# A spectral filter and two mixtures on one core: the first mixture's product with w_k in seven block products over pairs of chunks

## The chip, the cores and the metric

One core of a Trainium2 chip runs the whole kernel as one launch. The metric is the time of the device in microseconds (us). Lower is better.

## What is computed

The reference has three parts, one after the other, all in float32, for x of 8 batches, 3072 positions and 256 channels:

```python
y = irfft(rfft(x, axis=1) * (filt_r + 1j * filt_i), n=3072, axis=1)

prev = y moved by one position, 0 in front
xk = mu_k * y + (1 - mu_k) * prev
xr = mu_r * y + (1 - mu_r) * prev
k = relu(xk @ w_k)                      # 256 x 1024
x2 = sigmoid(xr @ w_r) * ((k * k) @ w_v)    # 256 x 256, 1024 x 256

h = max(x2 @ w1, x2 @ w2, x2 @ w3)      # 256 x 768 each
out = h @ w_out                         # 768 x 256
```

## The kernel before

**Products.** An fp32 product is made of three matmuls of a rounded type (fp32r): each operand is split into a hi and a lo part, and hi x hi, hi x lo and lo x hi are added up in a bank of PSUM (`mm3`, lines 155 to 163). `split` (line 177) makes the parts: ScalarE casts the hi part, and GpSimd (or VectorE, where it is named) subtracts it from the source for the lo part. Line 153 is the one line that issues every matmul, so the profile's groups are told apart by tile names.

**The transform** of a batch (`fft`, from line 328) runs in steps of small products through two buffers in DRAM, s1 and s2: 17 pieces that read x and write s1 (tiles xa, pa, ao), then 28 that read s1 (xb, pb), multiply with the filter, and write s2 (pc, co). Batch 0 has a version of its own (`fft_first`, line 420), in which the orders of TensorE, ScalarE and the DMA queue of SyncE are written by hand. Between its steps it also starts the conversion of the weights, which come as 64-bit numbers: a job is a triple of load, narrow (ScalarE, five VectorE operations, GpSimd) and parts. `CONV` and `LOAD` say at which step which job runs.

**The first mixture** works on chunks of 4 x 96 = 384 positions, 64 chunks in all. `y_load` and `y_mm` (lines 572, 583) bring a chunk's last transform step (py, yt) and make xk and xr (xm, then parts xh and xl). `r_mm` (line 613) makes the gate. `k_mm` (line 623) makes one of eight blocks of 128 columns of k: six matmuls, relu on ScalarE, the square on VectorE, the split. `v_mm` (line 636) follows three blocks behind: six matmuls into the two banks pv, with w_v's parts from DRAM. The parts of w_k stay on the chip. `x2` multiplies v by the gate.

**The second mixture** (`second`) takes two chunks at a time. `combos` (line 655) makes the sums of x2 that a product of 2 x 2 blocks by seven block products needs (Winograd's form), `block` (line 683) does the seven products of one of nine blocks (three fq, three of w1, w2 and w3), with the sums of the weights read from DRAM (wud). In it bank b collects products 1, 2, 4 and 6, and ScalarE copies it between them (pa, u, v); bank a takes product 3, bank e products 5 and 7. `out` takes the maximum (m), and `o_mm` (line 754) does the product with w_out in three banks po that stay open through the stage.

**The order.** The stages are lists of units with weights. In the steady part a pair of chunks is: first mixture of an even chunk, second mixture, first mixture of an odd chunk, sums. `drive` (line 108) lays the pieces of the next batch's transform between the units in proportion to their weights. Outside the hand-written parts the framework's planner then orders each engine's instructions by a simulated timeline. All tiles of PSUM come from one pool of eight banks (tag pm). Weights from DRAM go through one ring of buffers (`ws`), asked for eight loads ahead in the order of `later` and `piece_of` (lines 256 to 267), on SyncE's queue.

## Time and profile before

| | us |
|---|---|
| median of 3 runs | 3241.59 (3240.01 to 3244.37) |
| the profiled execution | 3234.65 |
| its span, first to last instruction | 3232.9 |
| TensorE busy in the span | 3117.1 (96%) |
| ScalarE / GpSimd / VectorE busy | 1918.4 / 1870.1 / 1839.3 |
| data moved by DMA | 676.38 MB |

The profile is one execution. PE is TensorE's matmuls, PEld its weight loads, DVE VectorE, ACT ScalarE, POOL GpSimd, SP SyncE. Times in a group are the sum of its busy time, the mean of one instruction in ns, and the idle time of the engine just before them with what ended it. Matmuls are pipelined, so the recorded length of one is longer than the distance to the next.

### The profile page before, as it was taken

How to read it: one execution, taken by the hardware profiler on the slowest of the kernel's cores; microseconds unless marked ns; L12 is line 12 of the kernel's file. 1: busy time of each engine (PE TensorE's matmuls, PEld its weight loads, DVE VectorE, ACT ScalarE, POOL GpSimd, SP SyncE). 2: the span in 40 equal slices, each digit the busy share in tenths (PEclk: the TensorE clock that was granted, in tenths of full speed). 3: DMA queues.
4: the chain of work that ended last, by engine and by line, in shares of the span. 5: the costliest groups of instructions: out<-in, count | busy, mean ns of one | idle time of the engine just before them, and what ended most of it. 6: DMA issues, size and time to landing. Idle time of an engine off the chain costs nothing.

```text
span 3232.9 us, 55814 instructions
## 1 busy us (share of the span) xinstructions
PE 3117.1 (96%) x19256; PEld 3040.1 (94%) x19256; DVE 1839.3 (57%) x2882; ACT 1918.4 (59%) x4024; POOL 1870.1 (58%) x1619
## 2 busy tenths in 40 slices
PE   7799899999999999999999999999999999999998
PEld 4799899999999999999999999999999999999998
DVE  4865565566555665566545565556654566555554
ACT  5556556666656666656666556565656566555554
POOL 3545665666555775556656566566665566544443
PEclk8899999999999999999999999999999999999999
DMA  8767786667765776657766677666776667655553
GB/s 283 234 227 218 246 298 186 193 200 245 225 195 183 230 225 204 208 185 243 233 191 189 206 241 233 192 185 203 254 226 192 190 211 226 190 171 159 163 167 119
DMA packets 397783, 676.38 MB, mean 209 GB/s; under 512 B 41920, under 2 KB 153664, under 8 KB 396864
## 3 DMA queue, kind: packets, MB, share of 16 engines
q1 hardware_dynamic: 328336, 585.61, 58.4%
q10 hardware_dynamic: 66752, 78.75, 7.1%
q0 software_dynamic: 2416, 8.46, 0.9%
q8 instruction: 156, 2.56, 0.3%
q14 instruction: 123, 1.01, 0.1%
HBM read 580.51 MB, written 92.14 MB: 208 GB/s over the span
## 4 chain that ended last, share of the span: by engine, by line
PE 82%; DMA 7%; DVE 6%; issue 2%; POOL 2%; ACT 1%; SPq 0%; ACTq 0%; POOLq 0%; DVEq 0%
PE pb L153 17%; PE pk L153 15%; PE pv L153 14%; PE po L153 12%; PE pe L153 8%; PE pa L153 7%; PE pr L153 4%; DMA ws<-wud 3%; PE py L153 3%; PE pc L153 2%; DVE xm L604 1%; POOL klo L179 1%; DMA xb<-s 1%; DVE sc L662 1%; DMA s<-ao 1%
## 5 line engine op out<-in xcount | busy, mean ns | idle before, releaser
L153 PE MATMUL pb<-x,ws 128*128 128x384 f32 x3456 | 749.1, 338 | 23.4 <-ACT v L698 8.4
L179 POOL TENSOR_TENSOR hh<-m,hh 128x384 fp32r<-128x384 f32 x384 | 400.5, 1048 | 610.6 <-ACT hh L178 497.4
L179 POOL TENSOR_TENSOR klo<-kr,khi 128x384 fp32r<-128x384 f32 x492 | 515.6, 1056 | 208.7 <-ACT khi L178 192.0
L153 PEld LDWEIGHTS pb<-x,ws 128*128 128x128 f32 x3456 | 595.9, 188 | 38.4 <-ACT v L698 10.5
L630 DVE SCALAR_TENSOR_TENSOR kr<-pk,kr 128x384 f32<-128x384 f32 x512 | 281.1, 552 | 489.5 <-ACT kr L629 489.4
L153 PE MATMUL pv<-khi,ws 128*128 128x384 f32 x2048 | 480.7, 337 | 6.7 <-ACT khi L178 6.7
L153 PE MATMUL po<-wo_hi,hh 128*128 128x256 f32 x2304 | 480.9, 283 | 3.8 <-ACT hh L178 2.8
L153 PE MATMUL pe<-x,ws 128*128 128x384 f32 x1728 | 389.8, 338 | 14.2 <-DVE m L737 10.7
L153 PEld LDWEIGHTS po<-wo_hi,hh 128*128 128x128 f32 x2304 | 391.1, 190 | 7.0 <-ACT hh L178 5.1
L153 PEld LDWEIGHTS pv<-khi,ws 128*128 128x128 f32 x2048 | 360.0, 188 | 11.6 <-ACT khi L178 10.1
L178 ACT CAST khi<-kr 128x384 fp32r<-128x384 f32 x512 | 261.0, 512 | 164.9 <-DVE kr L630 148.3
L153 PE MATMUL pk<-xh,wk_hi 128*128 128x384 f32 x1024 | 342.0, 337 | 3.9 <-ACT xh L178 3.9
L153 PE MATMUL pk<-xl,wk_hi 128*128 128x384 f32 x1024 | 344.3, 336 | 0.2 <-DVE xl L179 0.2
L153 PE MATMUL pk<-xh,wk_lo 128*128 128x384 f32 x1024 | 344.0, 336 | 0.0
L745 DVE TENSOR_TENSOR m<-sc,m 128x384 f32<-128x384 f32 x384 | 315.6, 828 | 7.3
L153 PEld LDWEIGHTS pe<-x,ws 128*128 128x128 f32 x1728 | 300.4, 189 | 20.1 <-DVE m L737 12.1
L153 PE MATMUL po<-wo_lo,hh 128*128 128x256 f32 x1152 | 317.0, 282 | 0.0
L629 ACT ACTIVATE kr<-pk 128x384 f32<-128x384 f32 x512 | 250.0, 489 | 109.9 <-PE pk L153 49.0
L178 ACT CAST hh<-m 128x384 fp32r<-128x384 f32 x384 | 194.7, 514 | 200.2 <-DVE m L745 142.2
L153 PE MATMUL pv<-klo,ws 128*128 128x384 f32 x1024 | 300.3, 339 | 10.0 <-POOL klo L179 8.9
L179 POOL TENSOR_TENSOR xl<-xm,xh 128x768 fp32r<-128x768 f32 x126 | 235.6, 1883 | 67.4 <-ACT xh L178 64.7
L604 DVE SCALAR_TENSOR_TENSOR xm<-yt,nmu_s,xm 128x384 f32<-128x384 f32 x256 | 210.7, 857 | 97.1 <-ACT xm L603 96.9
(129 smaller groups left out, 6065.9 us busy)
## 6 DMA issues: line engine op xcount, KB each, us to landing
ws<-wud SPq DMA_DIRECT2D x864, 256.0 KB, 3.4
ws<-wvd SPq DMA_DIRECT2D x512, 256.0 KB, 3.5
filt<-in_filt SPq DMA_DIRECT2D x84, 512.0 KB, 5.4
ws<-wud SPq DMA_DIRECT2D x288, 128.0 KB, 3.4
wbc<-wbcd SPq DMA_DIRECT2D x72, 512.0 KB, 4.7
cin<-s SPq DMA_DIRECT2D x64, 384.0 KB, 4.2
out_dram<-osb ACTq DMA_DIRECT2D x192, 128.0 KB, 3.1
xb<-s SPq DMA_DIRECT2D x85, 256.0 KB, 3.5
```

Source lines behind the costliest of these rows:

```text
L153: nc.tensor.matmul(o, lhsT=wgt, rhs=rhs, start=start, stop=stop, skip_group_check=more)
L178: nc.scalar.copy(hi, src)
L179: (lo_eng or nc.gpsimd).tensor_tensor(lo, src, hi.bitcast(F32), ALU.subtract)
L604: nc.vector.scalar_tensor_tensor(v[:, h], yt[:, h, :, :MC], nmu_s[:, w, h : h + 1], v[:, h], ALU.mult, ALU.add)
L629: nc.scalar.activation(r, p, AF.Relu)
L630: nc.vector.scalar_tensor_tensor(r, p, 0.0, r, ALU.max, ALU.mult)
L662: eng.tensor_tensor(t, a, b, ALU.subtract)
L745: nc.vector.tensor_tensor(m, c, m, ALU.max)
```

## The change

The first mixture takes pairs of chunks too. `combos` is made general (for `xk` and `x2`), and so is the code of the seven products (`seven`): `k_block` does one of four blocks of 256 columns of w_k for two chunks. Two of its four outputs are relu and square as before, the other two are first a sum of a bank and a copy, then relu and square on ScalarE. The sums of w_k are made during the transform of batch 0 (`block_job`, which had served w1 to w3) and are read from DRAM for each pair. `v_half` does half of a v product; w_v is loaded once for both chunks, and v has four banks. The units of a block of k are laid between the v halves of the block before; the last block's v halves go into the first block of the second mixture, and the y and r units of the pair after next into its blocks 0, 2, 3, 5, 6 and 7. The order is now: first mixture of pair p+1, second mixture of pair p, with the sums of x2 for p+1 after the first block of pair p+2. The transform's side list has a pause of weight 6 after the first load of its second step. Some buffers change in number (ws, xh, xl, yt, khi, klo, gate).

```diff
...
-    ws = ctx.enter_context(tc.tile_pool(name="ws", bufs=10))
+    ws = ctx.enter_context(tc.tile_pool(name="ws", bufs=9))
...
+    eye = cpool.tile([P, 2, P], F32, name="eye")
+    nc.scalar.dma_start(eye, ones)
...
+    wk_d = [dp.tile([P, 7, 2, P], F32, tag=f"wkd{k}", name=f"wkd{k}", bufs=1) for k in range(NF // 2)]
...
-        fq, j = divmod(k, 3)
+    def block_job(src, kt, q, to, queue):
...
+                queue.dma_start(to[:, a:e], t.bitcast(F32))
+        return piece(src, kt, 0, 2, 2 * P * q, 2 * P * (q + 1), parts)
...
-    wk = weight("wk", w_k, 2, DF)
...
-    wjobs1 = wk[2] + [wv_job(q) for q in range(NF // 2)] + wr[2]
+    wjobs1 = [block_job(w_k, 2, q, wk_d[q], nc.gpsimd) for q in range(NF // 2)] + wr[2]
+    wjobs1 += [wv_job(q) for q in range(NF // 2)]
...
+            if s == 0:
+                pieces.append((6.0, lambda: None))
             pieces.append((0.65, pc))
...
                 jobs[k][1](False)
-                jobs[k][2](False)
...
+            if s in CONV or s == 11:
+                jobs[CONV.get(s, 5) - 1][2](False)
...
-            e = mp.tile([NQ, C], F32, tag="cprev", name="cprev", bufs=1)
+            e = mp.tile([NQ, C], F32, tag="kr", name="cprev")
...
-        yt = mp.tile([P, 2, NP, MC + 1], F32, tag="yt", name="yt")
+        yt = mp.tile([P, 2, NP, MC + 1], F32, tag="yt", name="yt", bufs=1)
...
+            nc.gpsimd.tensor_copy(yt[:, :, :, 0], cs["y"])
+        if (i + 1) % NCH:
+            cs["y"] = mp.tile([P, 2, NP], F32, tag="yl", name="ylast", bufs=1)
+            nc.gpsimd.tensor_copy(cs["y"], yt[:, :, :, MC])
...
+            v = mp.tile([P, 2, NP, MC], F32, tag="xm", name="xm", bufs=3)
...
+            v = v.rearrange("p h t m -> p h (t m)")
+            if name == "k":
+                cs["k", i] = v
+            else:
+                hi = mp.tile([P, 2, NT], F32R, tag="xh", name="xh", bufs=1)
+                lo = mp.tile([P, 2, NT], F32R, tag="xl", name="xl", bufs=1)
+                split(hi, lo, v)
+                cs["r", i] = hi, lo
...
-        g = mp.tile([P, 2, NT], F32, tag="gate", name="gate", bufs=3)
...
-    def k_mm(i, f):
-        xh, xl = cs["k", i]
...
-        mm3(p, [(wk[0][:, k, s], wk[1][:, k, s]) for k in range(2)], [(xh[:, k], xl[:, k]) for k in range(2)])
-        r = mp.tile([P, NT], F32, tag="kr", name="kr")
-        nc.scalar.activation(r, p, AF.Relu)
-        nc.vector.scalar_tensor_tensor(r, p, 0.0, r, ALU.max, ALU.mult)
-        hi = mp.tile([P, NT], F32R, tag="khi", name="khi", bufs=LAG + 1)
-        lo = mp.tile([P, NT], F32R, tag="klo", name="klo", bufs=LAG + 1)
-        split(hi, lo, r, nc.vector if i == 0 or i < 4 and f % 2 else None)
...
+    def v_half(c, f, h, first, last, at):
+        kh, kl = cs["s", c, f]
+        if first:
+            cs["pv", c, h] = ps.tile([P, NT], F32, tag="pm", name="pv")
+        p = cs["pv", c, h]
         w = piece_of(at)
-        for h in range(2):
-            p = cs["pv"][h]
-            s = slice(h * P, (h + 1) * P)
-            mm(p, w[:, 0, s], kh, f == 0, False)
-            mm(p, w[:, 1, s], kh, False, False)
-            mm(p, w[:, 0, s], kl, False, f == NF - 1)
+        s = slice(h * P, (h + 1) * P)
+        mm(p, w[:, 0, s], kh, first, False)
+        mm(p, w[:, 1, s], kh, False, False)
+        mm(p, w[:, 0, s], kl, False, last)
...
-            nc.vector.tensor_tensor(g[:, h], cs["pv"][h], g[:, h], ALU.mult)
...
+            nc.vector.tensor_tensor(g[:, h], cs["pv", i % 2, h], g[:, h], ALU.mult)
+    def combos(name, ga, gb):
...
-            t = mp.tile([P, 2, NT], F32R, tag=f"x2_{k}", name="x2", bufs=1)
+            t = mp.tile([P, 2, NT], F32R, tag=f"{name}_{k}", name=name, bufs=1)
             split(t[:, 0], t[:, 1], v, eng)
-            cs["x2", k] = t[:, 0], t[:, 1]
+            cs[name, k] = t[:, 0], t[:, 1]
...
-    def block(p, k, at):
...
+    def comb_k(p):
+        combos("xk", cs.pop(("k", 2 * p)), cs.pop(("k", 2 * p + 1)))
+    def comb_x2(p):
+        combos("x2", cs.pop(("g", 2 * p)), cs.pop(("g", 2 * p + 1)))
+    def seven(name, at, out):
         st = {}
         def prod(o, n, onto):
             t = piece_of(at[n][0])[:, at[n][1]]
-            mm3(o, [(t[:, 0], t[:, 1])], [cs["x2", n]], onto, True)
+            mm3(o, [(t[:, 0], t[:, 1])], [cs[name, n]], onto, True)
...
-        def seven():
...
+        return [one, two, three, four, five, six, last]
+    def k_block(k, at):
+        def out(n, q, add=None):
+            r = mp.tile([P, NT], F32, tag="kr", name="kr")
+            if add is None:
+                nc.scalar.activation(r, q, AF.Relu)
+                nc.vector.scalar_tensor_tensor(r, q, 0.0, r, ALU.max, ALU.mult)
+            else:
+                c = mp.tile([P, NT], F32, tag="sc", name="sc", bufs=4)
+                nc.vector.tensor_tensor(c, q, add, ALU.add)
+                nc.scalar.activation(r, c, AF.Relu)
+                nc.scalar.activation(r, r, AF.Square)
+            hi = mp.tile([P, NT], F32R, tag="khi", name="khi", bufs=6)
+            lo = mp.tile([P, NT], F32R, tag="klo", name="klo", bufs=6)
+            split(hi, lo, r)
+            cs["s", n // 2, 2 * k + n % 2] = hi, lo
+        return seven("xk", at, out)
...
+    def u_block(k, at):
+        fq, j = divmod(k, 3)
...
+    def y_units(p):
+        i = 2 * p
+        return [
+            (0.0, lambda: y_load(i)),
+            (1.3, lambda: (y_mm(i), y_load(i + 1))),
+            (1.95, lambda: r_mm(i)),
+            (1.3, lambda: y_mm(i + 1)),
+            (1.95, lambda: r_mm(i + 1)),
+            (0.0, lambda: comb_k(p)),
+        ]
...
+    def kv(p, before=(), y=(), after=()):
...
+        for k in range(NKB + 1):
+            if k < NKB:
+                ask(wk_d[k], at[k], 0, 2)
+            if k:
+                av[2 * k - 2] = later(wv_d[k - 1][:, 0], 2, C)
+            if k < NKB:
+                ask(wk_d[k], at[k], 2, 4)
+            if k:
+                av[2 * k - 1] = later(wv_d[k - 1][:, 1], 2, C)
+            if k < NKB:
+                ask(wk_d[k], at[k], 4, 5)
+                ask(wk_d[k], at[k], 5, 7)
+        order = [(0, 0), (1, 1), (0, 1), (1, 0)]
+        for k in range(NKB + 1):
+            fill = []
+            if k:
+                for c, f in order:
+                    first = k == 1 and (c, f) in order[:2]
+                    end = k == NKB and (c, f) in order[2:]
+                    f += 2 * k - 2
+                    for h in range(2):
+                        fill.append((0.52, lambda c=c, f=f, h=h, first=first, end=end: v_half(c, f, h, first, end, av[f])))
+                    if end:
+                        fill.append((0.0, lambda c=c: x2(2 * p + c)))
+            else:
+                fill = before
+            if k == NKB:
+                return u, fill
+            for fn in k_block(k, at[k]):
+                u.append((0.52, fn))
+                if fill:
+                    u.append(fill.pop(0))
+            u += fill
+            u += y[2 * k - 2 : 2 * k] if k else list(after)
+    def second(p, before=()):
...
+        todo = list(before)
+        y = dict(zip((0, 2, 3, 5, 6, 7), y_units(p + 2))) if 2 * p + 4 < NTOT else {}
...
+            if k in y:
+                u.append(y[k])
...
+            now = u_block(k, at[k])
...
+                for _ in range(3 if k == 0 else n in ((3,), (0, 2, 3), (0, 1))[k % 3]):
+                    if todo:
+                        u.append(todo.pop(0))
...
+            if k == 0:
+                u += todo
+                todo = []
...
+        late = [(0.52, fn) for fn in late]
+        return u, late, [(0.71, lambda q=q: o_mm(p, NU // 2 - 1, q)) for q in range(2 * NTB)]
...
-        mm(p, wk[0][:, 0, :P], wk[0][:, 0, :NT], True, True)
-    wjobs1[8][0]()
+        mm(p, wr[0][:, 0, :P], wr[0].rearrange("p k n -> p (k n)")[:, :NT], True, True)
     y_mm(0)
-    eye = mp.tile([P, 2, P], F32, tag="osb", name="eye")
-    nc.sync.dma_start(eye, ones)
-    for k in (5, 6, 7, 8):
+    y_load(1)
+    r_mm(0)
+    y_mm(1)
+    comb_k(0)
+    r_mm(1)
+    for k in range(5, 9):
+        if k > 6:
+            wjobs1[k][0]()
         wjobs1[k][1]()
         wjobs1[k][2]()
...
-    units = kv(0) + kv(1) + kv(2) + [(0.0, lambda: combos(0))] + kv(3)
...
+    sums = lambda p: [(0.0, lambda: comb_x2(p))]
+    units, tail = kv(0, y=y_units(1)[:4])
+    first2 = len(units)
+    units += tail + y_units(1)[4:]
+    u, tail = kv(1, after=sums(0))
+    units += u
...
+    starts = [0]
+    for p in range(NPAIR):
+        if (2 * p + 4) % NCH == 0 and 2 * p + 4 < NTOT:
+            starts.append(len(units))
+        u, late, left = second(p, tail)
+        units += u
+        if p + 2 < NPAIR:
+            u, tail = kv(p + 2, late + left, after=sums(p + 1))
+            units += u
+        elif p + 1 < NPAIR:
+            units += late + sums(p + 1)
+            tail = left
+    units += late + left
+    lead2 = (first2 + 2 * before2) // 3
...
+            drive(part, side, sum(w for w, _ in part), sum(w for w, _ in side))
...
```

## Rows read from the trace of the kernel before

**Rows 1.** The page: the span, and busy time, share and instructions of each engine.
```profile
span 3232.9 us, 55814 instructions
...
PE 3117.1 (96%) x19256; PEld 3040.1 (94%) x19256; DVE 1839.3 (57%) x2882; ACT 1918.4 (59%) x4024; POOL 1870.1 (58%) x1619
```

**Rows 2.** Windows: stretch, busy time per engine (instructions), granted clock, DMA share, GB/s.
```profile
0.00:100.00 100.00, 64.82 (x197) 42.46 (x198) 48.90 (x69) 45.98 (x73) 43.63 (x42) 0.83 0.88 282
...
2800.00:2900.00 100.00, 100.00 (x635) 100.00 (x634) 52.09 (x87) 57.57 (x126) 49.44 (x46) 1.00 0.55 165
...
1180.00:1192.00 12.00, 12.00 (x75) 12.00 (x74) 3.58 (x7) 8.08 (x18) 10.08 (x9) 1.00 0.64 209
...
1216.00:1228.00 12.00, 11.02 (x69) 10.70 (x68) 7.91 (x15) 5.62 (x15) 3.60 (x4) 1.00 0.87 307
```

**Rows 3.** The chain that ended last: start, length in us, what.
```profile
140.00 3.12 PE ps L153 x28
...
2891.83 3.12 PE pk L153 x18
...
2978.69 3.12 PE pk L153 x18
```

**Rows 4.** Waits of TensorE, 600 to 3100 us: total us, times, longest.
```profile
PE pe L153 <- DVE m L737: 8.8, 6, 1.5
PE pv L153 <- POOL klo L179: 8.5, 12, 1.1
PE pb L153 <- ACT v L698: 8.4, 6, 1.7
PE pb L153 <- DMA ws<-wud: 5.4, 8, 1.4
PE pa L153 <- DMA ws<-wud: 5.2, 8, 1.0
PE pb L153 <- PE pe L153: 3.8, 6, 0.6
```

**Rows 5.** Groups: one of the three kinds of k matmul.
```profile
L153 PE MATMUL pk<-xh,wk_hi 128*128 128x384 f32 x1024 | 342.0, 337 | 3.9 <-ACT xh L178 3.9
```

**Rows 6.** TensorE's timeline at the start of the first mixture: start, us, what.
```profile
98.14 3.70 PE L153 MATMUL py<-wi_s,cin 96*128 96x96 f32 x16 [12.34 <-DMA cprev<-s]
...
106.57 1.65 PE L153 MATMUL pk<-xh,wk_hi 128*128 128x384 f32 x4 [3.87 <-ACT xh L178]
```

**Rows 7.** DMA: the total, then issues with their count, size and us to landing.
```profile
DMA packets 397783, 676.38 MB, mean 209 GB/s; under 512 B 41920, under 2 KB 153664, under 8 KB 396864
...
ws<-wvd SPq DMA_DIRECT2D x512, 256.0 KB, 3.5
...
cin<-s SPq DMA_DIRECT2D x64, 384.0 KB, 4.2
```

**Rows 8.** Groups of VectorE: a product and a sum out of PSUM, a sum in SBUF.
```profile
L630 DVE SCALAR_TENSOR_TENSOR kr<-pk,kr 128x384 f32<-128x384 f32 x512 | 281.1, 552 | 489.5 <-ACT kr L629 489.4
...
L744 DVE TENSOR_TENSOR sc<-pe,u 128x384 f32<-128x384 f32 x192 | 106.2, 553 | 69.5 <-PE pe L153 68.5
...
L662 DVE TENSOR_TENSOR sc<-gate 128x384 f32<-128x384 f32 x32 | 44.6, 1394 | 0.0
```

**Rows 9.** ScalarE's timeline where the transform of a batch starts its second step.
```profile
1410.85 0.62 ACT L178 CAST xbh<-xb 128x512 fp32r<-128x512 f32 x1 [2.51 <-DMA xb<-s]
1411.38 0.47 ACT L698 COPY v<-pb 128x384 f32<-128x384 f32 x1
1411.74 0.48 ACT L698 COPY u<-pb 128x384 f32<-128x384 f32 x1
```

**Rows 10.** Groups of ScalarE: the relu of k and one of the three copies.
```profile
L629 ACT ACTIVATE kr<-pk 128x384 f32<-128x384 f32 x512 | 250.0, 489 | 109.9 <-PE pk L153 49.0 <-POOL klo L179 41.5 <-POOL xbl L179 7.4
...
L698 ACT COPY u<-pb 128x384 f32<-128x384 f32 x288 | 138.7, 481 | 76.2 <-PE pb L153 75.4
```

**Rows 11.** Groups of GpSimd: the lo parts of k.
```profile
L179 POOL TENSOR_TENSOR klo<-kr,khi 128x384 fp32r<-128x384 f32 x492 | 515.6, 1056 | 208.7 <-ACT khi L178 192.0 <-DMA ws<-wud 6.9 <-PE pv L153 3.3
```

More of the change, by code (lines that the diff above doesn't have):

```diff
@@ L750, in out @@
                 cs["h", fq, n // 2, n % 2] = t
-        return [one, two, three, four, five, six, seven]
+        return seven("x2", at, out)
     def o_mm(p, fq, k):
@@ L812, in second, with ask @@
-    def second(p):
+    def ask(d, at, a, e):
+        i = later(d[:, a:e], e - a, 2, P)
+        at.update({n: (i, n - a) for n in range(a, e)})
+    def y_units(p):
[9 more added lines that the diff above has]
+    def kv(p, before=(), y=(), after=()):
+        u = []
+        before, y = list(before), list(y)
+        NKB = NF // 2
+        at = [{} for _ in range(NKB)]
+        av = {}
+        for k in range(NKB + 1):
[32 more added lines that the diff above has]
+            u += y[2 * k - 2 : 2 * k] if k else list(after)
@@ L902, in tile_spectral_moe @@
         part = units[starts[b] : ends[b]]
+        if b == 0:
+            for _, fn in part[:lead]:
+                fn()
+            part = part[lead:]
         if b + 1 < B:
             side = fft(b + 1)
-            cut = cuts[b] + n2 - starts[b]
-            if b == 0:
-                for _, fn in part[:lead]:
-                    fn()
-                part, cut = part[lead:], cut - lead
-            drive(part[:cut], side, sum(w for w, _ in part[:cut]), sum(w for w, _ in side))
-            for _, fn in part[cut:]:
-                fn()
+            drive(part, side, sum(w for w, _ in part), sum(w for w, _ in side))
         else:
```

111 lines of the change are left out of this document (15 added, 96 removed).

## The prediction

> **What bounds the kernel now.** I read the engine totals first [rows 1]: TensorE is busy for 3117.1 of 3232.9 us, and no other engine is above 59%. Then the windows [rows 2]: the first 100 us hold only 65 us of TensorE work at a granted clock of 0.83, and a window late in the run, where no transform runs beside the mixtures, is full (100.00 of 100) at clock 1.00. So the time is TensorE's stream of matmuls plus a start-up of its own kind. The price of a matmul comes from the chain in order of time [rows 3]: 18 matmuls of 384 columns take 3.12 us, so one takes 0.1733 us, and two pieces of the same place in the loop lie 86.83 us apart (2978.69 less 2891.83): one pair of chunks without a transform. The per-instruction mean of 335 to 338 ns in the groups is the length of a pipelined record, about twice the spacing; it must not be used as the price.
>
> The waits of TensorE between 600 and 3100 us [rows 4] sum to 40.1 us in 2500: the steady part is 98.4% full. About half of it lies, by the timeline, where the first mixture of an odd chunk hands over to the second mixture: late lo parts of k (8.5 us) and late w1/w2/w3 products from DRAM (5.4 + 5.2 us). The rest is one place per batch where ScalarE holds a copy back (8.4 us) and one where VectorE does (8.8 us), with 3.8 us put down to its own earlier products.
>
> **The change, part by part.**
>
> *w_k by seven block products.* A pair of chunks needed 2 x 8 x 6 = 96 matmuls of 384 columns; the groups have 1024 of each of three kinds [rows 5], 3072 in 32 pairs. Now four blocks of 7 x 3 = 21 make 84. Removed: 12 x 32 = 384, times 0.1733 us: **66.6 us** off the full engine. The number of v products stays (48 a chunk); only their order and the banks change.
>
> *Preparing the sums of w_k.* Four jobs are added, each of 28 matmul records like the preparation of w1 in the same chain: 3.12 us each [rows 3], 12.5 us, in the transform of batch 0, where TensorE's order is written by hand and was free of such work. TensorE has holes there, so not all of it is paid. Bounds 0 and 12.5; I take **+8**, nearer the upper end, since the order is fixed and each job's matmuls wait for its own conversion.
>
> *The start of the first mixture.* Before, the first k product starts 8.4 us after the first y product (106.57 less 98.14) [rows 6]. Now the sums xk need both chunks: y of chunk 1 waits for its load into a single buffer (`cin`, 4.2 us to landing [rows 7]) and for the one `yt` to come free, then four sums in a row on VectorE (0.55 to 1.39 us each [rows 8]) come before the second product. The r products of both chunks (24 x 0.1733 = 4.2 us) move there and fill part. The first block has nothing between its products. Lower end: one load, paid back by the r products, 0. Upper end: the load, the 8.4 us from y to the first product once more, and four sums at 1.39 us, 18. The four w_v jobs now all stand behind y, and the first v product waits for them. I take **+8**, near the middle, as the load is certain and the sums may hide behind r.
>
> *Handing over between stages.* The last v products of a pair now run among the first products of the second mixture, and the sums x2 are made a whole stage before they are used, so the two waits that made up 19.1 us (8.5 + 5.4 + 5.2 [rows 4]) lose their place. Late k parts can still occur, since the same four-step chain stands behind each v product; I take **-15**, bounds 0 and -19. The side work gets a pause of weight 6 between its first and second step: there the transform reads back what it has just written, and ScalarE stands 2.51 us at the cast of it before it comes to a copy that TensorE needs [rows 9]; of the 8.4 us of such copies I take **-6**, bounds 0 and -8.4.
>
> *ScalarE in a k block.* An output now costs more there: per block three copies out of PSUM, two relus from PSUM, two relus and two squares out of SBUF, four casts: 13 instructions, where the same 7.8 us of TensorE (21 + 24 matmuls, 45 x 0.1733) held 7.5. In the timeline [rows 9] two copies start 0.36 us apart, though the groups record 0.48 or 0.49 for each [rows 10]; with 0.4, an estimate for the mix with the longer casts, 13 make 5.2 us of 7.8, 67%, with the transform's casts and those of x2 on top. The window of today's first mixture shows 8.08 of 12 us, that of the second 5.62 [rows 2]. ScalarE stays under TensorE, but each product on bank b waits for a copy of it, as in the second mixture today. The waits there that name copies, sums and earlier products (8.8 + 8.4 + 3.8 = 21 us [rows 4]) fell in about 26 stages of 9 blocks (2500 us at some 97 us a pair), 0.09 us a block; for the 128 new blocks **+12**, bounds 0 (v products between them give more cover than today's) and 50 (0.4 us, one ScalarE place, in each).
>
> *VectorE.* Two of the four outputs of a block now take a sum out of PSUM (0.553 us) where they took a product out of PSUM (0.552) [rows 8]: nothing changes. The sums for xk are new: 7 instructions a pair (four sums, three lo parts), between 0.55 us (the PSUM form) and 1.39 us (the same form with both inputs in SBUF), 3.9 to 9.8 us, and they stand in the last three of nine blocks of the second mixture, together with the x stage of a chunk. The 0.55 would be the price without GpSimd beside it. VectorE has the cover on average (57%), but it is there that it holds TensorE back today. I take 0.3 us a pair, **+10**, bounds 0 and 62 (2.0 us a pair; the longest such wait of today is 1.5 [rows 4]).
> The page "SBUF — State Buffer" of the Trainium skill, section "Who interferes with whom", says that a VectorE instruction with two SBUF inputs and a GpSimd instruction that reads SBUF exclude each other for the whole instruction. The trace agrees (1394 ns against 553); by that rule the xk sums cost GpSimd their length too, which is the second rival.
>
> *GpSimd.* The lo parts of k (1056 ns [rows 11]) stay 16 a pair; for the x of k four of that size replace two of twice the elements, beside TensorE: costed at nothing. Where this cover is gone it shows as a wait for klo.
>
> *DMA.* w_v once a pair: 256 of 512 loads of 256 KB go, 67 MB. w_k comes in: 32 x 4 blocks of 7 x 128 KB, 117 MB; with 676 MB before [rows 7], +7%. SP issues 60 weight loads a pair for 52. The first mixture's demand goes from 4.2 MB in the time of 192 matmuls (33.3 us, 126 GB/s) to 5.8 MB in that of 180 (31.2 us, 185 GB/s), still under the 307 GB/s of a window of the second [rows 2]. One `ws` buffer fewer leaves eight loads ahead. Costed at nothing; without that cover a late load is 0.65 us on the mean and 1.4 at most [rows 4].
>
> The sum: -66.6 + 8 + 8 - 15 - 6 + 12 + 10 = -49.6 us. It is made on the profiled execution (3234.65 us, 1.75 us around its span), which is 7 us under the median of the three runs shown; against that median, 3241.59, it gives **3192 us**.
>
> **The rivals.**
>
> *The dovetailing takes all.* The preparation fits the holes and no new wait appears: -66.6 + 4 - 19 - 8.4 = -90, 3152 us. For it: late windows show the engine 100.00% full with the same kind of blocks. Against it: ScalarE and VectorE get some 17% and 12% more work (25 instructions of 0.4 us and 7 of about 1 us a pair).
>
> *VectorE and GpSimd at the end of the second mixture.* If the seven xk sums run at 1.39 us and the outputs of block 6 and 7 queue behind them, banks stay taken and TensorE stops about 2 us a pair: +62 in place of +10, 3244 us, no change. For it: VectorE waits are the largest entry of today's list [rows 4]. Against it: two blocks of the second mixture still lie between these sums and their first use, and each of today's waits is one per batch, not per pair.
>
> *PSUM, on the slow side.* From the second block on, v holds four of the pool's eight banks, and b and e of the last block with b and a of the new one are the other four; the transform needs one as well. Bank b comes free a relu and a product after the sixth product (0.49 [rows 10] + 0.55 us [rows 8], with a place in the queue 1.4), and product seven with two v parts (9 matmuls) cover 1.56. If ScalarE is three instructions behind (1.2 us), TensorE stops for about 1.05 us in 96 blocks: +101 in place of +12, 3281 us, slower. It decides from (49.6 + 12 + 6.5) / 96 = 0.71 us a block. Against it: the second mixture of today holds three banks of `po` besides its blocks and stops little.
>
> That the products don't fall away can't be: the three kinds of `pk` matmul are gone from the code.
>
> **How the numbers follow.** The forecast as summed, 0.49; all taken, 0.27; VectorE, 0.15; PSUM, 0.09. A measurement here tells 0.2%, 6.5 us, from no change. Faster by more: 0.49 + 0.27 and 0.07 of the VectorE case, **0.83**; within: 0.06 of that case; slower: 0.02 of it and PSUM, **0.11**. The range runs from 3150 (the first rival) to 3240 (preparation and start-up at their upper bounds, +14.5, none of the hand-over waits gone, +21, and 0.7 us a pair for the xk sums, +12); outside lie PSUM, half of the VectorE case and a little below, 0.2.
>
> **What would show it.** Right: `pk` records are replaced by 2688 in banks of b, a and e, TensorE's busy time falls by about 54 us, klo and `ws` waits fall under 10 us together, ScalarE rises to about 70% of the span. Wrong: a wait for a copy or a bank that comes back four times a pair (PSUM); waits for `m` in the last blocks of the second mixture (VectorE); the first block of k more than 30 us later than 106 us (start-up). A pair without transform that takes more than 86 us instead of 84.8 (86.83 less 12 x 0.1733) would refute the main term.

## The result and the profile after

The changed kernel takes 3285.97 us (median of four runs, 3283.08 to 3292.98) against 3240.8 us for the kernel before in the same comparison: a ratio of **1.0143 (95% interval 1.0131 to 1.0156)**, so 1.4% slower. 3192 us was forecast. The profiled execution of the changed kernel took 3292.98 us, 7 us over its median, and that of the kernel before 7 us under its own; so the two spans (3291.2 and 3232.9 us) differ by 58.3 us where the medians differ by 45.

The totals of the changed kernel's page, beside [rows 1]:

```profile
span 3291.2 us, 57217 instructions
...
PE 3108.8 (94%) x18984; PEld 2995.3 (91%) x18984; DVE 2063.2 (63%) x3086; ACT 2241.3 (68%) x4830; POOL 1982.0 (60%) x1765
```

272 matmuls fell away (384 less 112 of the w_k preparation), yet TensorE's busy time fell by 8.3 us only. A matmul's record is longer than its spacing (some 337 ns against 174 for 384 columns), and a short stall inside a string of them is counted as busy. So I priced every matmul at the median distance from its start to the next start (384 columns 0.1735 us, 256 columns 0.119, the transform's 512 columns 0.234, y 0.111, preparation 0.112), called the sum *work*, and what is left of the time up to the last matmul *lost*:

| | work | lost | of it up to 500 us | 500 to 2800 | behind |
|---|---|---|---|---|---|
| before | 3033.8 | 193.2 | 115.7 | 66.7 | 10.8 |
| changed | 2979.7 | 305.7 | 156.8 | 126.2 | 22.7 |
| difference | -54.1 | +112.5 | +41.1 | +59.5 | +11.9 |

The work fell by 54 us, which is the removed products and the whole of the preparation (-66.6 + 12.5), and twice as much was lost again: 41 us in the start, 60 us in the steady part. The Trainium skill's page "Perfetto Trace Analysis", section "Identifying the Most-Contended Engine", says that matmul busy time is not a good measure of how close a kernel is to the limit, because matmuls are pipelined, and names the rate of work done (MFU) and the weight loads' busy time in its place. This case agrees for the latter: PEld fell by 44.8 us and came far nearer the 54.1.

TensorE's waits between 600 and 3100 us in the changed kernel (total, times, longest), beside [rows 4]:

```profile
PE pr L153 <- ACT xh L180: 10.9, 14, 1.3
PE pe L153 <- DVE sc L771: 9.1, 10, 1.1
PE po L153 <- POOL hh L181: 8.2, 9, 1.2
PE pe L153 <- DVE m L768: 8.1, 8, 1.2
PE pb L153 <- DMA wbc<-wbcd: 6.9, 13, 1.1
PE pr L153 <- DMA ws<-wud: 5.4, 4, 1.4
PE pc L153 <- DVE m L764: 4.6, 6, 0.8
```

The waits for klo are gone, and those for w1/w2/w3 are down from 10.6 us to 5.4, as forecast. New are the r products waiting for xh, products of bank e waiting for VectorE (L768 and L771 are the outputs of a block of the second mixture), `po` waiting for h at the hand-over, and the transform's products waiting for its weights. By the place of the lost time, 40 us of 600 to 2800 us lie around the third block of the second mixture, where the change puts y and r of the first chunk (nothing there before), 20 us in the eighth and ninth, behind the xk sums (13 before), and 37 us in the first mixture (1.4 us there before). The first two blocks, where klo and a part of the weights were waited for, lose 1 us in place of 24, and the fourth 6 in place of 18.

The start, in TensorE's timeline, beside [rows 6]; and the windows of that stretch:

```profile
115.87 3.70 PE L153 MATMUL py<-wi_s,cin 96*128 96x96 f32 x16 [9.20 <-DMA cprev<-s]
...
128.11 1.01 PE L153 MATMUL pr<-xh,wr_hi 128*128 128x384 f32 x2 [7.68 <-ACT xh L180]
...
142.42 1.01 PE L153 MATMUL pr<-xh,wr_hi 128*128 128x384 f32 x2 [6.69 <-ACT xh L180]
143.23 1.16 PE L153 MATMUL pb<-xk,ws 128*128 128x384 f32 x3
```

```profile
100.00:125.00 25.00, 9.52 (x36) 8.47 (x36) 19.31 (x27) 8.77 (x18) 13.60 (x13) 0.63 0.79 261
125.00:150.00 25.00, 14.65 (x49) 13.63 (x50) 21.62 (x29) 12.68 (x24) 14.18 (x12) 0.50 0.33 100
```

The first y product comes 17.7 us later than before (115.87 against 98.14), and from there to the first k product it takes 27.4 us where it took 8.4. Behind the idle stretches the granted clock is down to 0.50, the lower of its two levels (1.2 of 2.4 GHz), so what does run there runs slowly: the r products from 132.65 us on start 0.32 us apart, where 0.1735 is the price elsewhere. VectorE is the busiest engine of the second 25 us (21.62).

### The profile page after: what moved, and what is told of

Read it like the earlier page. It is cut to its first block, busy times and chain, and to the rows that moved or that the text cites. A ratio compares the mean times of both kernels' runs of the same rounds, so it can differ in the third digit from the quotient of the medians.

```text
span 3291.2 us, 57217 instructions
## 1 busy us (share of the span) xinstructions
PE 3108.8 (94%) x18984; PEld 2995.3 (91%) x18984; DVE 2063.2 (63%) x3086; ACT 2241.3 (68%) x4830; POOL 1982.0 (60%) x1765
## 4 chain that ended last, share of the span: by engine, by line
PE 73%; DVE 11%; DMA 7%; ACT 4%; issue 3%; POOL 1%; ACTq 0%; SPq 0%; POOLq 0%; DVEq 0%
PE pb L153 23%; PE pv L153 14%; PE pe L153 10%; PE po L153 10%; PE pa L153 7%; PE pr L153 4%; PE py L153 2%; PE pc L153 2%; DMA wbc<-wbcd 2%; DVE xm L613 2%; DVE m L772 1%; DVE sc L660 1%; DMA wbc<-in_wbc 1%; DVE sc L771 1%; DVE m L768 1%
## 5 line engine op out<-in xcount | busy, mean ns | idle before, releaser
L181 POOL TENSOR_TENSOR klo<-kr,khi 128x384 fp32r<-128x384 f32 x512 | 536.9, 1059 | 292.2 <-ACT khi L180 180.7
L181 POOL TENSOR_TENSOR hh<-m,hh 128x384 fp32r<-128x384 f32 x384 | 425.0, 1117 | 224.4 <-ACT hh L180 196.6
L153 PE MATMUL pv<-khi,ws 128*128 128x384 f32 x2048 | 449.3, 336 | 9.8 <-ACT khi L180 9.8
L772 DVE TENSOR_TENSOR m<-sc,m 128x384 f32<-128x384 f32 x384 | 388.9, 1013 | 8.9
L153 PEld LDWEIGHTS pv<-khi,ws 128*128 128x128 f32 x2048 | 360.0, 188 | 13.1 <-ACT khi L180 11.9
L153 PE MATMUL pb<-xk,ws 128*128 128x384 f32 x1536 | 351.3, 341 | 10.6 <-ACT pa L706 2.5
L153 PEld LDWEIGHTS pb<-xk,ws 128*128 128x128 f32 x1536 | 273.0, 191 | 21.8 <-ACT co L410 4.3
L701 ACT COPY u<-pb 128x384 f32<-128x384 f32 x416 | 199.4, 479 | 117.8 <-PE pb L153 113.5
L153 PE MATMUL pv<-klo,ws 128*128 128x384 f32 x1024 | 267.8, 336 | 0.0
L701 ACT COPY v<-pb 128x384 f32<-128x384 f32 x416 | 198.8, 478 | 100.7 <-PE pb L153 98.5
L706 ACT COPY pa<-pb 128x384 f32<-128x384 f32 x416 | 196.6, 473 | 58.4 <-PE pb L153 47.6
L153 PEld LDWEIGHTS po<-wo_lo,hh 128*128 128x128 f32 x1152 | 219.7, 191 | 0.3
L153 PE MATMUL pa<-x,ws 128*128 128x384 f32 x864 | 200.0, 335 | 0.0
```

The lines of the kernel that those rows point to most:

```text
L153: nc.tensor.matmul(o, lhsT=wgt, rhs=rhs, start=start, stop=stop, skip_group_check=more)
L181: (lo_eng or nc.gpsimd).tensor_tensor(lo, src, hi.bitcast(F32), ALU.subtract)
L701: nc.scalar.copy(st[to], st[of])
L706: nc.scalar.copy(st["a"], st["b"])
L772: nc.vector.tensor_tensor(m, c, m, ALU.max)
```

## The experiments

Every ratio is to the kernel before on the same chip. Differences between two other runs are of their medians; by the ratios they come out up to 6 us otherwise (43 becomes 37, 30 becomes 25). Three theories stood at the beginning: A, VectorE's instructions with both inputs in SBUF are slowed by GpSimd; B, the new k blocks (ScalarE's copies, four banks of v); C, the y and r stages are laid too close together among the blocks of the second mixture.

**A shorter VectorE at the outputs.** Sum and maximum of a second-mixture output go through PSUM. The sum is written back, so bank e carries the added copy on into the seventh product.

```
-                c = mp.tile([P, NT], F32, tag="sc", ...)
-                nc.vector.tensor_tensor(c, q, add, ALU.add)
-                nc.vector.tensor_tensor(m, c, m, ALU.max)
+            if add is not None:
+                nc.vector.tensor_tensor(q, q, add, ALU.add)
+            nc.vector.tensor_tensor(m, q, m, ALU.max)
```

> The sum of a bank and a copy in the second mixture is written back into its bank, so that the maximum after it reads one operand from PSUM and one from SBUF: 384 VectorE instructions lose their second SBUF input, the count of instructions stays. Theory A (after the first 500 us, VectorE's instructions with two SBUF inputs wait behind trains of GpSimd instructions, and TensorE waits for them): the 1013 ns of these maxima fall to about 560, TensorE's waits for sc and m (23 us between 600 and 3100 us) mostly go, 20 to 40 us faster than the changed kernel, 3246 to 3266 us. Theory B (the k blocks themselves, by ScalarE's copies and the four banks of v): within 5 us of 3286. Theory C (the y and r stage laid among the second mixture, a chain too short in distance): a gain under 10 us.

3310.66 us, ratio 1.0208 (1.019 to 1.0225). The group of the maximum, first in the changed kernel, then here:

```profile
L772 DVE TENSOR_TENSOR m<-sc,m 128x384 f32<-128x384 f32 x384 | 388.9, 1013 | 8.9
```

```profile
L769 DVE TENSOR_TENSOR m<-pe,m 128x384 f32<-128x384 f32 x384 | 212.7, 554 | 9.1
```

and TensorE's waits here, between 600 and 3100 us:

```profile
PE pb L153 <- DVE m L769: 22.9, 18, 1.6
...
PE pc L153 <- DVE m L769: 8.7, 6, 1.5
PE pe L153 <- DVE m L769: 8.1, 16, 0.6
```

The instruction is 0.46 us shorter, VectorE 161 us less busy, and the kernel 25 us slower. Mean 1013 ns with both inputs in SBUF and 554 ns with one in PSUM agree with the Trainium skill's page "SBUF — State Buffer", section "Who interferes with whom", by which a VectorE instruction with two SBUF inputs contends with a GpSimd instruction that reads SBUF, and one with at most one SBUF input does not. But what was bought with it was a bank held longer: `pb` and `pc`, which read nothing that this instruction makes, now wait for it. So a shorter instruction alone doesn't help, and banks came up as a suspect. What A costs by itself the run doesn't show, since it brought this wait of its own.

**The new order without the seven-block products.** The k products are direct again (three kinds, one bank each), in the order of the change; the weight buffers go from 9 to 8 (one load fewer asked for ahead), the sums' from 4 to 3 and khi's and klo's from 6 to 5, to make room for w_k.

```
-            for fn in k_block(k, at[k]):
-                u.append((0.52, fn))
+            for fn in k_block(k):
+                u.append((1.04, fn))
```

> The new order of the stages is kept, but the product with w_k is direct again: 24 matmuls a block in place of 21, w_k's parts on the chip, no sums of x or w_k, no copies (two buffers of khi and klo, one of ws and one of sc fewer, seven loads ahead). TensorE's work rises by 54 us (66.6 less the 12.5 of the preparation). Theory B: the waits of the steady part fall back to those of the kernel before (-70) and the start with them (-30): about 3240 us. Theory A: the seven sums of xk go, a third of the waits with them (-25), start -30: about 3285. Theory C: the waits stay, only the start improves: about 3310 us.

3290.06 us, ratio 1.0142 (1.012 to 1.0163): the same as the change. Its work is that of the kernel before (3033.8 us), and it loses 253 us. So **the order, with these buffers, costs about 46 us without the seven-block products**, and they give nothing net: they save 54 us of work and lose 53 more (306 against 253 us). Of the three forecasts that of A is nearest (about 3285), by which a third of the waits would go with the sums of xk; this run takes out the sums, the copies and the preparation at once and doesn't tell which of them the 53 us are. The waits, 600 to 3100 us:

```profile
PE pa L153 <- DVE m L774: 19.2, 5, 3.8
PE pb L153 <- DMA wbc<-wbcd: 12.6, 10, 1.8
PE pk L153 <- DVE filt L398: 10.9, 18, 1.0
```

`pk` has no input from the transform's `filt`; it waits for a bank that this VectorE instruction still reads.

**r two or three blocks behind y.**

```
-        y = dict(zip((0, 2, 3, 5, 6, 7), y_units(p + 2)))
+        y = dict(zip((0, 1, 3, 4, 7, 6), y_units(p + 2)))
```

The y products and the xk sums come a block earlier by the same edit.

> Inside the second mixture the y units move to blocks 0, 1, 3, 4, 7 and 6, so that two or three blocks lie between a y product and the r product that needs its x, in place of one, and the xk sums come a block earlier. Theory C: TensorE's waits for xh (10.9 us between 600 and 3100 us) go, 10 to 20 us faster: 3266 to 3276. Theory A: those of VectorE stay, 5 to 10 us faster at most. Theory B: no change.

3269.08 us, ratio 1.0079 (1.006 to 1.0098), 17 us less than the change. The wait of r for xh left the list. By the tally of the table, the lost time around the third block went from 42 us to nothing, but that of the seventh to ninth rose from 26 to 45: much of it only moved. Two y stages of the same place in the loop, late, where no transform runs, in TensorE's timeline; first the changed kernel:

```profile
2927.58 0.69 PE L153 MATMUL py<-wi_s,cin 96*128 96x96 f32 x5
...
3015.30 0.47 PE L153 MATMUL py<-wi_s,cin 96*128 96x96 f32 x3
```

and here:

```profile
2905.42 0.58 PE L153 MATMUL py<-wi_s,cin 96*128 96x96 f32 x4
...
2990.08 0.69 PE L153 MATMUL py<-wi_s,cin 96*128 96x96 f32 x5
```

A pair takes 87.72 us in the change and **84.66 us** here; 84.8 was forecast. So the main term can be had, and these late pairs had lost 3 us each to the order.

**The change without its pause.** The three lines with the weight of 6 go.

> The pause of weight 6 between the transform's two steps is taken out. If the pause does what it is for: one wait of about 1.6 us per batch for the read-back comes back, 7 batches: 10 us slower, 3296. If its price is higher than its gain (the second step's pieces are pressed into less time, and its loads of wbc come late, 6.9 us between 600 and 3100 us, none before): 0 to 10 us faster.

3329.12 us, ratio 1.0257 (1.0232 to 1.0283): the pause is worth 43 us in the new order, where the prediction gave it 6 and the expectation 10. The waits are those of bank e for VectorE; why they grow without the pause is not shown:

```profile
PE pe L153 <- DVE m L761: 23.1, 23, 1.5
PE pe L153 <- DVE sc L741: 12.7, 15, 2.2
```

**One PSUM bank fewer, in both kernels.** Now theory D, that the new order has no bank to spare.

```
-    ps = ctx.enter_context(tc.tile_pool(name="ps", bufs=8, ...))
+    ps = ctx.enter_context(tc.tile_pool(name="ps", bufs=7, ...))
```

> The changed kernel with seven PSUM banks in place of eight. Theory D (the new order needs more banks at one time in the second mixture: y, r, the transform and three banks of po beside the block, so that a bank is not free when its first product is due): one bank fewer costs 60 us or more, over 3345 us, and far more than in the kernel before. Theory C (the loss is the short distance of the y and r stages in the second mixture, not banks): under 25 us, below 3310 us.

> The kernel before with seven PSUM banks in place of eight. Theory D: the old order has a bank to spare, under 15 us, below 3259 us. If the old order loses as much as the new one by a bank, banks are no more the bound of the new order than of the old one, and D falls.

The changed kernel: 3374.34 us, 1.0407 (1.0391 to 1.0422), 88 us over the change. The kernel before: 3225.74 us, **0.9952 (0.9937 to 0.9967), faster** with seven. In the new order:

```profile
PE pe L153 <- DVE m L764: 31.3, 25, 2.4
```

That the new order leans on the eighth bank and the old one doesn't is shown. That it loses time for want of a ninth is not; no run has one.

**r in the second mixture, in the kernel before.**

```
-        if i > 0:
+        if i > 0 and (i < 4 or i % 2 == 0):
             add(1.95, r_mm, i)
...
+            if k == nb - 2 and p and i < NTOT:
+                add(1.95, r_mm, i)
```

> The kernel before, with the r products of every second chunk moved from the start of its first mixture to the last block but one of the second mixture before it, one block behind their y stage, which is where the change has them. Theory C (y and r in the second mixture are paid for beside the transform): half of the change's r stages move, 10 to 20 us slower than before, 3254 to 3264 us, with waits of pr for xh. Theory D: one bank more for a short time, a few us. Theory E (the w_k sums alone): no change, within 6 us of before.

3225.39 us, 0.9947 (0.9929 to 0.9965): 18 us faster. C as I had put it, that r among these blocks costs by itself, fell: one block behind y, as in the change, it cost nothing in the old order. So the distance alone doesn't make the price; what else stands there would have to count too, which this run doesn't show.

**Both together in the kernel before.**

> The kernel before with the r products of every second chunk in the second mixture and with seven PSUM banks: both runs by themselves came to 3225 us. If the r stage really uses a bank that the old order has to spare, then with seven it has none and the time rises to 3240 us or more (theory D in the old order). If both gains are independent, 3207 us; if both are the same shift of the transform's steps, 3220 to 3230 us.

3280.44 us, 1.0119 (1.0104 to 1.0134): two edits that each save 18 us cost 55 us over either together. The waits:

```profile
PE pr L153 <- ACT xh L178: 12.8, 12, 1.8
PE pr L153 <- DVE kr L630: 8.5, 12, 0.7
PE pk L153 <- DVE filt L391: 7.7, 12, 0.8
PE pc L153 <- DVE kr L630: 5.6, 12, 0.5
```

The last three name readers of other tiles, which I read as banks not yet free. They stand in the first mixture, not at the r products that were moved; so the old order comes to lean on the eighth bank too once r is moved; that the moved stage is what takes the bank is not shown.

**The w_k parts behind the first transform** (and r later, as above). Three of the four preparations are issued after batch 0's transform.

```
-            if s in CONV or s == 11:
+            if s in (0, 11):
                 jobs[CONV.get(s, 5) - 1][2](False)
...
+    for k in (1, 2, 3):
+        wjobs1[k][2]()
```

> The changed kernel with the y and r stages one block apart as in the run with r later (3269 us there), and the products of three of the four w_k preparations taken out of the hand-ordered transform of batch 0 and put behind it. Theory S (the preparation in that stretch delays the whole start): the first product of a k block comes 15 to 25 us earlier than at 143 us, and the time is 3244 to 3254 us. Rival (the start is bound by the chain from the transform's last store over y to the sums): first product within 5 us of 143 us, 3264 us or more.

3263.85 us, 1.0064 (1.0049 to 1.0079), 5 us less than with r later alone and outside what theory S forecast. The first k product comes at 129.18 us, 12 us earlier than there, but 24.4 us behind the first y product (104.74) still. The steady part keeps some 45 us of lost time around the seventh and eighth block of the second mixture (600 to 2800 us, by the tally of the table). VectorE's timeline shows what stands there:

```profile
1208.14 0.58 DVE L669 TENSOR_TENSOR sc<-xm 128x384 f32<-128x384 f32 x1
1208.65 0.54 DVE L772 TENSOR_TENSOR m<-sc,m 128x384 f32<-128x384 f32 x1
1209.12 0.55 DVE L660 TENSOR_TENSOR sc<-sc,xm 128x384 f32<-128x384 f32 x1
1209.58 1.36 DVE L660 TENSOR_TENSOR sc<-xm 128x384 f32<-128x384 f32 x1
1210.87 0.55 DVE L660 TENSOR_TENSOR sc<-xm,sc 128x384 f32<-128x384 f32 x1
...
1213.80 0.69 DVE L397 TENSOR_TENSOR filt<-pb,filt 128x512 f32<-128x512 f32 x1
1214.41 0.55 DVE L181 TENSOR_TENSOR xk<-sc,xk 128x384 fp32r<-128x384 f32 x1
1214.88 1.65 DVE L772 TENSOR_TENSOR m<-sc,m 128x384 f32<-128x384 f32 x1
...
1216.92 0.54 DVE L771 TENSOR_TENSOR sc<-pe,u 128x384 f32<-128x384 f32 x1
```

and TensorE's:

```profile
1217.52 0.79 PE L153 MATMUL pe<-x,ws 128*128 128x384 f32 x3 [1.07 <-DVE sc L771]
```

The sums of xk (L669, L660), two of their lo parts (L181) and three products of the transform (L397 is the last) run back to back from 1208.14, with outputs' sums and maxima among them; the last maximum shown takes 1.65 us, the sum of a later output (1216.92) comes behind it, and TensorE, whose bank e that sum reads, has stood for 1.07 us when it goes on at 1217.52.

**The xk sums in two pieces.** On that kernel; two sums and one of VectorE's three lo parts stay at the seventh block, the rest goes to the ninth (the parts are put in that order in x2 too). One of the two sums also moves from the ring of four `sc` buffers, which the outputs use, to another buffer.

```
-        y = dict(zip((0, 1, 3, 4, 7, 6), y_units(p + 2)))
+        y = dict(zip((0, 1, 3, 4, 7, 6, 8), y_units(p + 2)))
```

> The kernel of the run with the w_k parts late (3264 us), with the xk sums of a pair laid in two pieces, at the 7th and the 9th block of the second mixture, in place of one piece at the 7th. Theory V (the seven sums and parts in a row hold VectorE, and the sums of a block's outputs queue behind them): the loss in the blocks around them falls from 41 us to under 20, waits of pe for VectorE's sums fall under 8 us, the time is 3240 to 3252 us. Theory D (banks): the block behind keeps its waits, 3258 us or more.

**3234.18 us, 30 us less** and below the range given for theory V, ratio to the kernel before 0.9987 (0.9975 to 1.0). The 45 us of the seventh and eighth block fall to some 8, but the whole stretch from 600 to 2800 us loses only 18 us less (107 to 89 in the profiled executions, the later of which was 7.5 us above its median): 13 us are new around the first block, most of them y waiting for its load. The largest waits are:

```profile
PE py L153 <- DMA cin<-s: 7.9, 6, 1.8
PE pa L153 <- DVE m L784: 5.7, 5, 1.4
PE pb L153 <- ACT yt L602: 4.6, 6, 1.5
PE pe L153 <- DVE sc L760: 4.5, 4, 1.1
```

V holds for this order: the same instructions, laid in two pieces, give back the largest single amount of all runs that keep the change. The buffer that was freed by the same edit is a rival that no run tests by itself; against it, VectorE stands idle before none of the instructions shown above, so it waited for no buffer there. A pair without a transform takes more again in this run, 86.60 us from y at 2873.76 to y at 2960.36.

**y one block later still**, so that its load has two blocks (places 0, 2, 4, 5, 7, 6, 8).

> The kernel of the run with the sums split (3234 us), with the y stages one block later, so that the load of a chunk has two blocks before its first product in place of one. If the 7.9 us of waits for that load are time of the path: 3224 to 3230 us. If they only take the place of another wait: within 6 us of 3234 us.

3243.72 us, 1.0008 (0.9994 to 1.0021), 9.5 us more than with the sums split and outside both forecasts. The waits for the load went, and `po` waits 20.1 us for hh instead: another wait took their place.

**The pause, and nine weight buffers, each alone in the kernel before.**

> The kernel before, with the pause of weight 6 between the first and second step of the transform's second half and nothing else of the change. If the pause only spares the read-back of what was just written, the old order gains what the prediction gave it, about 6 us, and at most the 8.4 us of copies: 3235 to 3240 us. If it is worth 43 us in any order, 3200 us. If it is worth that only where banks are short (theory D), within 6 us of the kernel before.

> The kernel before with 9 weight buffers in place of 10, which is a part of the change by itself. The prediction costed it at nothing: within 6 us of the kernel before. If it is a part of the steady loss: 15 us or more slower, with waits for weights above 20 us between 600 and 3100 us. A difference as large in the other direction would say that the planned order moves the time by so much with no cause of its own.

3236.91 us, 0.9985 (0.9974 to 0.9997), and 3224.72 us, 0.9949 (0.9934 to 0.9964). The pause is worth 3 us there and 43 in the new order; its result lies in the range of two of the three cases of the expectation and doesn't tell them apart. A buffer less made the kernel 16 us *faster*, though the waits for weights rose to 20.3 us. With seven banks and with r moved, this is the third unrelated edit that ends near 3225 us: I read it as the planned order of instructions moving the time by half a per cent, and I don't explain differences of up to 18 us between two orders by the edit alone. By that measure the 17 us of r later are not clear of it, and the smaller gains below and above show no cause by their size.

**What the start pays for.** The products, copies and stores of the w_k preparation left out for three of four blocks (their conversions stay, and all blocks read the sums of the first); then, in both kernels, the conversion of three of the four parts of w_v.

```
-                jobs[CONV.get(s, 5) - 1][2](False)
+                if CONV.get(s, 5) - 1 in (0, 4):
+                    jobs[CONV.get(s, 5) - 1][2](False)
```

```
-    for k in range(5, 9):
...
+    wjobs1[5][1]()
+    wjobs1[5][2]()
```

> The changed kernel with the sums of w_k prepared for the first of its four blocks only: the conversions stay, but 84 small products, their copies and stores are left out, and all four blocks read the sums of the first, so three quarters of the keys are computed with the wrong weights. If the preparation costs what the prediction gave it (8 us for four, at most 12.5), 6 to 9.4 us come back, 3277 us or more, and the first product of a k block stays within 10 us of 143 us. If it is what delays the start, 20 us or more come back, 3266 us or less, with the first product before 125 us.

> The changed kernel with the first of the four parts of w_v converted and used for all four, so the second mixture's other keys meet the wrong w_v; the conversions of the other three, five VectorE instructions for each half, are left out of the start. Theory K (VectorE runs the weight conversions between the x steps of the second chunk, and so the chain from y to the sums of xk comes late): the first product of a k block comes 8 us or more earlier than 27 us after the first y product, and 10 to 30 us come back, 3256 to 3276 us. Rival (the chain of two chunks is long by itself): still 24 to 28 us from y to that product, under 8 us come back, 3278 us or more.

> The kernel before with the same left out. Theory K: in the old order one chunk was enough for the first product and the conversions stood behind it, so less comes back than in the changed kernel: under 10 us, 3231 us or more. If as much comes back here, the conversions are a price of both kernels and no part of what the change lost.

3279.11 us (1.0127, 1.0095 to 1.0159), 3278.26 us (1.0117, 1.0097 to 1.0138) and 3238.36 us (0.9989, 0.9978 to 1.0). Why w_v was tried shows in VectorE's timeline of the changed kernel, between the x steps (L613) of the two chunks:

```profile
124.31 2.88 DVE L613 SCALAR_TENSOR_TENSOR xm<-yt,nmu_s,xm 128x384 f32<-128x384 f32 x2
127.11 0.41 DVE L215 TENSOR_SCALAR we<-we 128x512 f32<-128x512 f32 x1
...
135.25 0.69 DVE L221 SCALAR_TENSOR_TENSOR wm<-wst,wm 128x512 f32<-128x512 uint32 x1
135.86 1.14 DVE L613 SCALAR_TENSOR_TENSOR xm<-yt,nmu_s,xm 128x384 f32<-128x384 f32 x2
```

For 8.7 us it converts weights (L215 to L221) before it comes to the x steps of the second chunk. Not all of that is a wait, since that chunk's y products only start at 128.91 us. Without three of the parts:

```profile
115.86 3.70 PE L153 MATMUL py<-wi_s,cin 96*128 96x96 f32 x16 [10.03 <-DMA cprev<-s]
...
135.41 1.16 PE L153 MATMUL pb<-xk,ws 128*128 128x384 f32 x3
```

The first k product comes 7.8 us earlier and 8 us come back, 4 us more than in the old order, which by its size alone is not clear of the noise between orders. It is about a fifth of what the start lost. The preparation gave 7 us for three of four blocks, as forecast. The chain of two chunks, 19.6 us here against 8.4, is the remainder, with its r products still 0.32 us apart; neither of the two rivals in the expectation is the whole. Neither the four sums nor the products of the w_k preparation are what makes it long in the change: in the run with direct w_k products, which has neither, the first k product still comes 27.0 us behind the first y product (119.44 less 92.49).

## Why the prediction was wrong, by its steps

The steps that failed are the start, the y and r stages, which had no term, and the first mixture.

- **w_k by seven block products, -66.6: right.** The work fell by it, and a pair without a transform takes 84.66 us once r is moved, against 86.86 before (the prediction's 86.83 is a slip: 2978.69 less 2891.83 is 86.86). The test given ("takes more than 86 us … would refute the main term") was drawn wrongly: the change took 87.72 us with the term intact, because another place lost 3 us a pair.
- **Preparing the sums of w_k, +8: right as far as can be told.** 7 us for three of four.
- **The start of the first mixture, +8 (0 to 18): failed.** From y to the first k product it is 19 us more, over the upper bound, and the first y product is 17.7 us late on top; the first 500 us lose 41 us more. The term left out that VectorE's queue holds the weight conversions as well (8 us), and that TensorE's granted clock is then down to 0.50 to 0.63, so that the r products that were to fill the time stand nearly twice as far apart. Why the first y product is late was not taken apart; with three w_k parts behind the transform it comes 10 us earlier (104.74 against 114.62 with r later alone).
- **Handing over between stages, -15: half right.** The klo waits went, and the first two blocks of the second mixture lose 23 us less; `po` for h (8.2 us) and the transform's weights (6.9 us), which no row of before held, came, much of them in the first mixture.
- **The pause, -6: right in sign.** 3 us in the old order. That it would be worth 43 us in the new order was not seen.
- **ScalarE in a k block, +12: right in size, by luck.** The lost time ahead of k-block products is about 12 us between 600 and 2800 us, but the waits of their bank b name the transform's copy `co` (2.4 us), VectorE's squares (1.3) and a weight load (0.5), and none a copy of the block, which was the mechanism of this term. The first mixture as a whole loses 36 us more than before. The PSUM rival, priced as a stop in each k block, did not happen.
- **The y and r stages in the second mixture: no term at all, and the largest place that was left out.** Nothing was put down for the chain y, copy, x step, cast that must end before r. Around the block with y and r of the first chunk the changed kernel loses 40 us, where the kernel before loses nothing in that block. With r two or three blocks behind y that went to nothing, but the time fell by 17 us only, as other blocks then lost more.
- **VectorE, +10 for the xk sums: near in the changed kernel, short of what this place can cost.** The eighth and ninth block lose 20 us against 13 before. With r later the blocks around the sums lose 45, and splitting the sums gave 30 us. The term looked at the user of the sums, two blocks away; who waits is the outputs of blocks queued behind them on the same engine. The rival that named this place had that mechanism, with 0.15; its 62 us did not come, though the sums took 1.17 us on the mean in the changed kernel, not far from its 1.39.
- **Banks.** Counted in the k blocks and not in the second mixture, where y, r, the transform and `po` meet. The change loses 88 us by a bank fewer; how much it loses with eight for want of a ninth can't be told.
- **The steady part, read as 98.4% full.** That came from the list of waits, 40.1 us between 600 and 3100 us; the tally of the table gives the kernel before 65 us lost there, so the waits that the terms were scaled from were too short.

By the tally the steady part (500 to 2800 us) loses 126 us in the change, 115 with r later, 113 with the w_k parts late as well and 92 with the sums split, against 67 before. So 34 of the 59.5 us came back in series; the other 25, and more than half of the 41 us in the start, are located but not taken apart, and their cause stays open.

What is faster than both kernels: the kernel before with every second chunk's r products moved (3225.39 us), though by no more than other orders of it are. The change with r later, the w_k parts late and the sums split stands 0.1% under the kernel before, with 1.0 the end of its interval.

## What to carry to other kernels

A saving on a full engine is only as good as the order that is rebuilt around it: for each step that is moved, price the chain that leads to it and the queue that it stands in, for the instructions behind it as well as for its own user. A string of instructions on a half-idle engine is worth laying in pieces. Before trusting a difference of half a per cent between two planned orders, make an edit that should do nothing.

## What was not expected of the hardware

TensorE's busy time hid the loss: it fell by 8 us while 54 us of work went and 112 us of lost time came. Between 600 and 2800 us the changed kernel's TensorE counts as idle for 71.7 us (2200 less 2128.28 busy), where the tally finds 121 lost. VectorE's maximum with both inputs in SBUF took 4.74 us four times, some 390 us apart (1290.02, 1678.35, 2066.66 and 2459.66). At the first of them GpSimd ran from one instruction straight into the next:

```profile
1290.02 4.74 DVE L772 TENSOR_TENSOR m<-sc,m 128x384 f32<-128x384 f32 x1
```

```profile
1290.17 0.54 POOL L604 COPY yt<-ylast 128x192 f32<-128x192 f32 x1
1290.57 1.84 POOL L181 TENSOR_TENSOR xl<-xm,xh 128x768 fp32r<-128x768 f32 x1
1292.37 1.01 POOL L181 TENSOR_TENSOR xk<-xm,xk 128x384 fp32r<-128x384 f32 x1
1293.33 1.01 POOL L181 TENSOR_TENSOR hh<-m,hh 128x384 fp32r<-128x384 f32 x1
```

The maximum ended at 1294.76, 0.4 us after the fourth of these. The means of 1 us in the groups hide such cases.
